# Linear attention and a mixture of experts on one core: unused keys left out, early chunks reordered, the expert choice and the small tiles' rows moved, last rows scaled by one engine

## The chip, the core and the metric

The kernel runs on one core of one Trainium2 chip. The time is device time in microseconds (us) from one launch; the median of several runs is compared. The engines of a core run their own queues of instructions in order: TensorE (PE; its weight loads are shown as PEld), VectorE (DVE), ScalarE (ACT), GpSimd (POOL) and SyncE (SP, which here issues nearly all transfers). An instruction that waits holds up everything behind it on its engine.

## The reference

Two stages, with the values of the first as the tokens of the second. First, causal linear attention with a decay per head (4 batches, 8 heads, 768 positions, 64 values a head):

```
for each block b of 64 positions:
    intra = ((qb @ kb.T) * Dmask) @ vb          # Dmask = lam ** (i - j), lower triangle
    inter = (qb * lam ** (pos + 1)) @ kv_state
    out[b] = intra + inter
    kv_state = lam ** 64 * kv_state + (kb * lam ** (63 - pos)).T @ vb
```

Then the 3072 tokens of 512 values go through 8 experts, each token through the one with the largest logit:

```
logits = x @ w_gate + modality_bias[modality_id]
e = argmax(logits);  gate = softmax(logits)[e]
out[token] = gate * (relu(x @ w1[e]) @ w2[e])    # w1: 512 x 1024, w2: 1024 x 512
```

## The kernel before

The attention works in chunks of 128 positions: 6 chunks a batch, 24 in all, taken in 12 pairs (pair m holds chunks 2m and 2m+1). `load(m)` brings the four inputs of a pair (keys turned, queries turned, values, keys in rows; 2 MB) into one of four buffers. For a chunk g, `scores` multiplies keys by queries for 8 heads, `mask` (L258, DVE, one instruction of 128x1024, tile `pt`) applies the decay, `query` (POOL) and `keys` (ACT, 8 small instructions, tile `kd`) scale queries and keys, `products` forms keys times values, `add` (DVE) rolls that into one of three states, `from_state` (L282) multiplies the scaled queries by the state, `values` (L293) the masked scores by the values, and ACT copies the result to `xt`. The last chunk of a batch (g % 6 == 5) has no `keys`, `products` and `add`, since no later chunk needs its state. `from_state` takes a list of chunks and steps through the head pairs p; for each p it does each chunk in turn, and `place` gives even and odd chunks opposite halves of the output's partitions, so that two chunks' four matmuls of 64x64 (one for each half of the heads) stand in four different quarters of the array:

```
        for p in range(NP):
            for g in both:
                if g % NC > 0:
                    for hl, r in enumerate(halves2):
                        nc.tensor.matmul(ops[g][place(g, hl), p, :], state[g % NC % 3][r, p, :], qds[g][r, p, :], ...
```

The results of `from_state` and of `turn` (L314, which transposes four chunks' `xt` into token rows, `grp`) share two PSUM buffers named `o`: a buffer is written again only when DVE (L321) and ACT (L323, two copies) have emptied it.

After pairs 3, 7 and 11 the routing of 8 chunks is made: `gates` (PE) gives logits, `gate_rows` (L358, DVE) transposes them, `choose` (L363) puts eight small instructions in a list `todo` (add the bias, maximum, two comparisons `eq`, `m8`, the one-hot `oh`, a subtraction, an exponential on ACT), and `do(n)` issues the next n of that list at fixed places. `ranks` (L381, PE) multiplies the one-hot by a triangle; its results give each token its slot, and POOL scatters the token rows to their experts' stretches of an array `placed`.

The second stage takes tiles of 256 tokens of one expert. `fetch_x`, `fetch_w1`, `fetch_w2` issue the transfers; `turn_rows` and `split_rows` (DVE, ACT) transpose a tile's rows (`xt`) and split them into a high and a low part; `split_w1` splits the first weights (`w1h` on ACT, `w1l` on DVE); `first_layer` multiplies on PE and splits the second weights meanwhile; `second(n, t)` does the second layer for half a tile, scales by the gate and scatters to the output. Tiles 0 to 3 come from early lists, tiles 6 to 13 are the fixed ones of the last list. Two small tiles (4 with up to 64 tokens, 5 with up to 32) are fitted in between: their rows are fetched (`xq`), turned by `thin_rows` (L630, DVE, tile `xf`, then one instruction for addresses, `to`), multiplied by `thin_first` (L727, PE, L737) between `second(n, 0)` and `second(n, 1)` of tiles 7 and 9, turned by `thin_turn` and finished by `thin_second` (PE, L764) inside the next tile's `first_layer`. PE, DVE, ACT and SP run in the order in which the code calls; POOL's order is tied by hand as well.

Of the kernel before, what the change touches and what calls it, by code (L numbers as in the profile page):

```python
# [18 lines left out]
NC = S // P  # L19
# [24 lines left out]
def linear_attention_moe(tc, qkv, lam, modality, wg, mbias, w1, w2, out):  # L44
    nc = tc.nc
    with ExitStack() as ctx:
# [38 lines left out]

        def load(m):
            halves[m] = slot([P, 4, HB, H * D], F32, "load")
            if m > 2:
                nc.sync.dma_start(out=halves[m], in_=source(m))
                return  # L90
            for c in range(HB):
                for part in ((slice(0, 2), slice(2, 4)) if m < 2 else (slice(0, 4),)):
                    nc.sync.dma_start(out=halves[m][:, part, c], in_=source(m)[:, part, c])

        for m in range(3):
# [121 lines left out]
        def query(g):  # L217

            if g % NC > 0:
                qds[g] = work.tile([P, NP, P], F32, name="qd", bufs=4)  # L220
                op = pool(nc.gpsimd.tensor_tensor(out=qds[g], in0=loaded(g)[1], in1=pq, op=ALU.mult))
                if g in begun:
                    after(op, begun.pop(g))
# [129 lines left out]
        def do(n=None):  # L353
            for what, args, kw in todo[:n]:
                what(*args, **kw)
            del todo[:n]
# [345 lines left out]
                                               op0=ALU.max, op1=ALU.subtract)  # L702
                between(i)

        def second(n, t, ticks=(1, 3, 5, 7), halved=False):
            idx = idxs[n]
            ts = slice(t * P, (t + 1) * P)
            yp = ps.tile([P, DM], F32, name="o", bufs=2)
            for f in range(FC):
                a, b = divmod(f, 2)  # L710
                mm = three(yp, hh[a // 2][:, a % 2, b, ts], hl[a // 2][:, a % 2, b, ts], w2h[a][:, b, :], w2l[a][:, b, :],
                           f == 0, f == FC - 1)
                if f in ticks:
                    tick(mm)
            y = work.tile([P, DM], F32, name="y", tag="qd", bufs=4)
            share = idx[:, t, 1:2].bitcast(F32)
            w = DM // 2 if halved else DM
            nc.scalar.activation(out=y[:, :w], in_=yp[:, :w], func=AF.Copy, scale=share)  # L718
            if halved:
                nc.vector.tensor_scalar(out=y[:, w:], in0=yp[:, w:], scalar1=share, scalar2=None, op0=ALU.mult)  # L720
            sc = nc.gpsimd.indirect_dma_start(  # L721
                out=out, out_offset=bass.IndirectOffsetOnAxis(ap=idx[:, t, 0:1], axis=0),
                in_=y, in_offset=None, bounds_check=N - 1, oob_is_err=False)
            apart("tokens", sc)
            pool(sc, free=True)
# [109 lines left out]
        scores(3)  # L835
        mask(3)
        query(3)
        gpsimd_constants()
        load(SLOTS)
        products(2)  # L840
        products(3)
        add(2)
        add(3)
        from_state((2, 3))
        values(2)
        values(3)
        block(4)
        turn(0, 0)
        turn(0, 1)
# [3 lines left out]
        turn(0, 3)  # L853
        load(1 + SLOTS)
        products(4)
        products(5)
        add(4)
        for m in range(2, pairs):
            a, b = HB * m, HB * m + 1
            ahead = m + 1 < pairs  # L860
            add(b)
            if ahead:
                block(a + 2)
                mm = block(b + 2)
                if m > 4:
                    tick(mm)
            if m == 2:
                routing_constants()
            elif m == 3:
                clear(slice(E * CAP, E * CAP + TT), TT)  # L870
            do(7)
            from_state((a, b))
            values(a)
            mm = values(b)
            if m == 5 or m == 9:
                jobs += [("slots", one_slot)] * RC
# [19 lines left out]
            if m % 2 and ahead:  # L896
                mm = turns(m // 2)
                if m > 4:
                    tick(mm)
            if m == 3 or m == 7:  # L900
                routed = m // 4, *choose(m // 4, gate_rows())
            do(3 + m % 2)
            if m == 8:
                need("slots")
                raw1 = w1_part("raw1", F32)
# [103 lines left out]
        for n in [3] + list(range(wides, fixed_ones)):  # L1009
            first_layer(between)  # L1010
            between = lambda i: None
            m = n + 1 if n > 3 else wides
            if m < fixed_ones:
                fetch_w2(*fetch_regs(m, m == wides))
                turn_rows(m)
                split_rows()
                if m + 1 < fixed_ones:
                    fetch_x(m + 1)
                split_w1()
                if m + 1 < fixed_ones:  # L1020
                    fetch_w1(*fetch_regs(m + 1))
            thin = {wides + 1: thins, wides + 3: thins + 1}.get(n)
            if thin:
                thin_rows(thin)
            second(n, 0)
            if thin:
                hn = thin_first(xf[thin], homes[thin][0])
            second(n, 1, halved=n + 1 == fixed_ones)
            if thin:
                hnt[thin] = thin_turn(hn)  # L1030
                between = finish(thin, 0)
            thin = {wides: thins, wides + 2: thins + 1}.get(n)
            if thin:
                fetch_x(thin)
                fetch_w1(*fetch_regs(thin, True), to=homes[thin][0])
                fetch_w2(*fetch_regs(thin, True), to=homes[thin][1])
# [68 lines left out]
```

## Time and profile before

| what | value |
|---|---|
| median of 3 runs | 407.89 us (405.15 to 409.21) |
| profiled execution, its own time | 407.92 us |
| its span (first to last instruction) | 406.2 us |
| PE busy | 385.9 us (95%) |
| DVE / ACT / POOL busy | 258.5 (64%) / 210.8 (52%) / 97.9 us (24%) |
| mean granted TensorE clock | 0.978 of full speed |
| moved by DMA | 83.77 MB, mean 206 GB/s |

The span is cut into stages with different limits, so the shares of busy time are averages. PE counts as busy while a matmul runs at whatever clock the throttle grants; a stretch at half clock is therefore not seen as idle. The view of waits tells for whom an engine sat idle; the timeline gives instructions in order of time with the idle time just before them and what ended it; the chain of waits follows the work back from the last instruction. In all of them an fp32 matmul leaves two records, so 8 instructions show as x16.

### The profile page before, as it was taken

The numbers are of one execution on the slowest core, as the hardware profiler recorded it, in microseconds if no ns is written. First come the engines' busy times: TensorE is split into PE (matmuls) and PEld (weight loads), VectorE is DVE, ScalarE is ACT, GpSimd is POOL, SyncE is SP. The second block draws the span as 40 slices with busy tenths as digits, with TensorE's granted clock in tenths as the row PEclk, the third lists the DMA queues.
The fourth block names the chain that finished last, engine by engine and source line by source line (L and its number), as shares of the span: only waits on it lengthen the run. The fifth ranks groups of instructions, "written<-read, shape, count | busy, mean of one in ns | idle before, by whom it ended". The sixth has DMA issues, their size and how long they took to land.

```text
span 406.2 us, 9717 instructions
## 1 busy us (share of the span) xinstructions
PE 385.9 (95%) x3602; PEld 339.7 (84%) x3602; DVE 258.5 (64%) x462; ACT 210.8 (52%) x411; POOL 97.9 (24%) x128
## 2 busy tenths in 40 slices
PE   8999799999999999999999959999959999999993
PEld 4889689888888989898989937889839989898982
DVE  5676859778576788866776651475742666758520
ACT  2477468775356465654655442364533365556420
POOL 2653219645502274010202010002011020100201
PEclk9999989999999999999999979999989999999997
DMA  7999868999769973799328995452930120210101
GB/s 252 388 400 406 329 243 284 399 333 314 208 180 312 361 237 121 292 358 319 82 54 260 341 362 217 129 165 77 395 79 27 24 57 27 64 42 2 53 0 50
DMA packets 41384, 83.77 MB, mean 206 GB/s; under 512 B 7278, under 2 KB 20078, under 8 KB 41328
## 3 DMA queue, kind: packets, MB, share of 16 engines
q1 hardware_dynamic: 37408, 70.28, 51.8%
q0 software_dynamic: 3920, 12.78, 8.2%
q8 instruction: 30, 0.49, 0.5%
q14 instruction: 26, 0.21, 0.2%
HBM read 90.57 MB, written 17.84 MB: 267 GB/s over the span
## 4 chain that ended last, share of the span: by engine, by line
PE 43%; issue 33%; DMA 9%; POOL 4%; DVE 4%; ACT 3%; SPq 2%; POOLq 0%; ACTq 0%; DVEq 0%
DMA load<-in_qkv_dram 5%; PE s L254 4%; PE o L298 4%; PE o L673 4%; PE o L675 4%; PE o L674 4%; POOL out_dram L721 4%; PE o L290 2%; PE o L317 2%; PE s L675 2%; PE s L674 2%; PE s L673 2%; ACT w1h L581 2%; PE s L693 2%; PE kv L693 2%
## 5 line engine op out<-in xcount | busy, mean ns | idle before, releaser
L582 DVE TENSOR_TENSOR w2l<-raw,w2h 128x1024 fp32r<-128x1024 f32 x48 | 58.7, 1224 | 40.2 <-ACT w2h L581 40.2
L721 POOL DMA_INDIRECT out_dram<-y,idx x24 | 29.6, 1234 | 226.0 <-ACT y L718 207.4
L673 PE MATMUL o<-w2h,hh 128*128 128x512 f32 x192 | 75.6, 394 | 0.0
L674 PE MATMUL o<-w2l,hh 128*128 128x512 f32 x192 | 75.0, 390 | 0.0
L675 PE MATMUL o<-w2h,hl 128*128 128x512 f32 x192 | 74.8, 390 | 0.0
L582 DVE TENSOR_TENSOR w1l<-raw,w1h 128x1024 fp32r<-128x1024 f32 x44 | 51.5, 1220 | 2.0 <-ACT w1h L581 2.0
L581 ACT CAST w2h<-raw 128x1024 fp32r<-128x1024 f32 x48 | 49.9, 1040 | 0.0
L673 PE MATMUL kv<-xh,w1h 128*128 128x256 f32 x176 | 49.7, 283 | 0.0
L673 PE MATMUL s<-xh,w1h 128*128 128x256 f32 x176 | 49.6, 282 | 0.0
L674 PE MATMUL s<-xl,w1h 128*128 128x256 f32 x176 | 49.5, 281 | 0.0
L674 PE MATMUL kv<-xl,w1h 128*128 128x256 f32 x176 | 49.4, 281 | 0.0
L675 PE MATMUL s<-xh,w1l 128*128 128x256 f32 x176 | 49.4, 281 | 0.0
L675 PE MATMUL kv<-xh,w1l 128*128 128x256 f32 x176 | 49.4, 281 | 0.0
L673 PEld LDWEIGHTS o<-w2h,hh 128*128 128x128 f32 x192 | 36.2, 188 | 8.3 <-issue 1.2
L581 ACT CAST w1h<-raw 128x1024 fp32r<-128x1024 f32 x44 | 42.8, 1044 | 0.0
L675 PEld LDWEIGHTS o<-w2h,hl 128*128 128x128 f32 x192 | 36.2, 188 | 7.7
L674 PEld LDWEIGHTS o<-w2l,hh 128*128 128x128 f32 x192 | 36.2, 189 | 7.1
L718 ACT ACTIVATE y<-o,idx 128x512 f32<-128x512 f32 (+1 forms) x24 | 16.2, 675 | 42.3 <-PE o L675 36.8
L236 ACT ACTIVATE kd<-load,dk 128x64 f32<-128x64 f32 x144 | 35.7, 338 | 3.3 <-DMA load<-in_qkv_dram 3.2
L673 PEld LDWEIGHTS kv<-xh,w1h 128*128 128x128 f32 x176 | 33.3, 189 | 0.6 <-issue 0.6
L674 PEld LDWEIGHTS s<-xl,w1h 128*128 128x128 f32 x176 | 33.2, 189 | 0.4
L673 PEld LDWEIGHTS s<-xh,w1h 128*128 128x128 f32 x176 | 33.2, 189 | 0.3
(191 smaller groups left out, 645.1 us busy)
## 6 DMA issues: line engine op xcount, KB each, us to landing
raw<-in_w_dram SPq DMA_DIRECT2D x96, 512.0 KB
load<-in_qkv_dram SPq DMA_DIRECT2D x9, 2048.0 KB
both<-in_w_dram SPq DMA_DIRECT2D x16, 512.0 KB
xg<-placed SPq DMA_DIRECT2D x48, 128.0 KB
placed<-blank SPq DMA_DIRECT2D x9, 528.0 KB
load<-in_qkv_dram SPq DMA_DIRECT2D x8, 512.0 KB
load<-in_qkv_dram SPq DMA_DIRECT2D x2, 1024.0 KB
placed<-grp,sloti POOLq DMA_INDIRECT x24, 6.2
```

What stands on the lines that cost most here:

```text
L236: nc.scalar.activation(out=kds[g][:, p, hl, :], in_=kn[:, p, hl, :], func=AF.Copy, scale=dk[:, hl, p, P - 1 : P])
L254: mm = nc.tensor.matmul(scs[g][:, hl, p, :], kt[r, p, :], qt[r, p, :], start=True, stop=True)
L290: nc.tensor.matmul(ops[g][place(g, hl), p, :], state[g % NC % 3][r, p, :], qds[g][r, p, :], start=(p == 0), stop=False)
L298: mm = nc.tensor.matmul(op[place(g, hl), p, :], vt[:, (2 * p + hl) * D : (2 * p + hl + 1) * D], pt[:, hl, p, :], start=(c == 0 and p == 0) ...
L581: nc.scalar.copy(out=hi, in_=src)
L582: nc.vector.tensor_tensor(out=lo, in0=src, in1=hi.bitcast(F32), op=ALU.subtract)
L673: nc.tensor.matmul(out, ah, bh, start=first, stop=False)
L674: nc.tensor.matmul(out, ah, bl, start=False, stop=False)
L675: return nc.tensor.matmul(out, al, bh, start=False, stop=last)
L693: mm = nc.tensor.matmul(hp[:, j, :], raw1[i][:, kc, fs], xt2[:, kc, :], start=(kc == 0), stop=(kc == KC - 1))
L718: nc.scalar.activation(out=y[:, :w], in_=yp[:, :w], func=AF.Copy, scale=share)
L721: sc = nc.gpsimd.indirect_dma_start(out=out, out_offset=bass.IndirectOffsetOnAxis(ap=idx[:, t, 0:1], axis=0), in_=y, in_offset=None, bound ...
```

## The change

Five edits.

1. `load`: of a pair whose second chunk is the last of a batch (m = 2, 5, 8, 11) that chunk's keys in rows are left out (0.25 MB each); such a pair comes in two transfers, one a chunk, where pairs 5, 8 and 11 came in one.
2. Chunks 2 to 5: `from_state` and `values` of chunk 2 stand behind `products(2)`, those of chunk 3 behind `products(3)`, those of chunk 4 ahead of the scores of chunks 6 and 7, each chunk alone; chunk 5 follows these scores, alone too.
3. `gate_rows` and `choose` of the first two routings go from the end of pairs 3 and 7 to the head of pairs 4 and 8, and all of `choose` is issued behind the masks of the next two chunks; `do` counts change to fit.
4. `thin_rows` goes from behind the next tile's `turn_rows`, `split_rows` and `split_w1` to ahead of them.
5. The last half tile's scaling, which ACT and DVE shared by halves, is done whole by ACT.

```
 def load(m):
     halves[m] = slot([P, 4, HB, H * D], F32, "load")
-    if m > 2:
+    last = (HB * m + 1) % NC == NC - 1
+    if m > 2 and not last:
         nc.sync.dma_start(out=halves[m], in_=source(m))
         return
     for c in range(HB):
-        for part in ((slice(0, 2), slice(2, 4)) if m < 2 else (slice(0, 4),)):
+        for part in ((slice(0, 2), slice(2, 4)) if m < 2 else (slice(0, 4 - (last and c)),)):
...
-            share = idx[:, t, 1:2].bitcast(F32)
-            w = DM // 2 if halved else DM
-            nc.scalar.activation(out=y[:, :w], in_=yp[:, :w], func=AF.Copy, scale=share)
-            if halved:
-                nc.vector.tensor_scalar(out=y[:, w:], in0=yp[:, w:], scalar1=share, scalar2=None, op0=ALU.mult)
+            nc.scalar.activation(out=y, in_=yp, func=AF.Copy, scale=idx[:, t, 1:2].bitcast(F32))
...
+        products(2)
         gpsimd_constants()
         load(SLOTS)
-        products(2)
+        from_state((2,))
+        values(2)
+        add(2)
         products(3)
-        add(2)
+        from_state((3,))
+        values(3)
         add(3)
-        from_state((2, 3))
-        values(2)
-        values(3)
         block(4)
...
         products(4)
-        products(5)
         add(4)
+        from_state((4,))
+        values(4)
         for m in range(2, pairs):
             a, b = HB * m, HB * m + 1
             add(b)
+            if m == 4 or m == 8:
+                routed = m // 4 - 1, *choose(m // 4 - 1, gate_rows())
             if ahead:
                 block(a + 2)
                 mm = block(b + 2)
...
-            do(7)
-            from_state((a, b))
-            values(a)
+            do(9 if m % 4 == 0 else 8)
+            if m > 2:
+                from_state((a, b))
+                values(a)
+            else:
+                from_state((b,))
             mm = values(b)
...
-            if m == 3 or m == 7:
-                routed = m // 4, *choose(m // 4, gate_rows())
-            do(3 + m % 2)
+            else:
+                do(4)
...
         for n in [3] + list(range(wides, fixed_ones)):
             first_layer(between)
             between = lambda i: None
+            thin = {wides + 1: thins, wides + 3: thins + 1}.get(n)
+            if thin:
+                thin_rows(thin)
             m = n + 1 if n > 3 else wides
             if m < fixed_ones:
                 fetch_w2(*fetch_regs(m, m == wides))
                 turn_rows(m)
                 split_rows()
...
                 split_w1()
...
-            thin = {wides + 1: thins, wides + 3: thins + 1}.get(n)
-            if thin:
-                thin_rows(thin)
             second(n, 0)
```

What stands on the engines, in the order in which they run it. First VectorE around tile 7, before (`hl` is the low part of the hidden values, `xt`, `xl`, `w1l` belong to the next wide tile, `xf` and `to` to the small one):

```order
L701 SCALAR_TENSOR_TENSOR hl_1800<-kv,hh_1798 128x512
L661 STREAM_TRANSPOSE xt_128<-xg 128x4x4x32 x2
L582 TENSOR_TENSOR xl_131<-xt_128,xh_129 128x512
L582 TENSOR_TENSOR xl_132<-xt_128,xh_130 128x512
L582 TENSOR_TENSOR w1l<-raw_1412,w1h 128x1024 x4
L661 STREAM_TRANSPOSE xf_3492<-xq_3260 128x2x4x32
L638 TENSOR_SCALAR to_3494<-idx_3259,strip 128x1
```

and now:

```order
L702 SCALAR_TENSOR_TENSOR hl_1802<-kv,hh_1800 128x512
L662 STREAM_TRANSPOSE xf_3421<-xq_3263 128x2x4x32
L639 TENSOR_SCALAR to_3423<-idx_3262,strip 128x1
L662 STREAM_TRANSPOSE xt_128<-xg 128x4x4x32 x2
L583 TENSOR_TENSOR xl_131<-xt_128,xh_129 128x512
L583 TENSOR_TENSOR xl_132<-xt_128,xh_130 128x512
L583 TENSOR_TENSOR w1l<-raw_1416,w1h 128x1024 x4
```

The two instructions of the small tile moved ahead of the eight of the next wide tile. The same move stands at tile 9.

Second, VectorE at the head of pair 4, before (`lgt` are the transposed logits, `state` the additions of `add(9)`, `pt` the masks of chunks 10 and 11, `m` and `oh` the end of the choice):

```order
L360 STREAM_TRANSPOSE lgt<-x 128x256
L355 TENSOR_TENSOR l<-lgt,bias 128x64
L355 TENSOR_REDUCE mx<-l 128x8
L355 TENSOR_TENSOR eq<-l,mx 128x64
L355 TENSOR_TENSOR eq<-eq,desc 128x64
L278 SCALAR_TENSOR_TENSOR state_122<-state_121,pq,kv 128x64 x4
L260 TENSOR_TENSOR pt<-s,dk 128x1024 x2
L355 TENSOR_REDUCE m_734<-eq 128x8
L355 TENSOR_TENSOR oh<-eq,m_734 128x64
```

and now:

```order
L279 SCALAR_TENSOR_TENSOR state_122<-state_121,pq,kv 128x64 x4
L361 STREAM_TRANSPOSE lgt<-x 128x256
L261 TENSOR_TENSOR pt<-s,dk 128x1024 x2
L356 TENSOR_TENSOR l<-lgt,bias 128x64
L356 TENSOR_REDUCE mx<-l 128x8
L356 TENSOR_TENSOR eq<-l,mx 128x64
L356 TENSOR_TENSOR eq<-eq,desc 128x64
L356 TENSOR_REDUCE m_739<-eq 128x8
L356 TENSOR_TENSOR oh<-eq,m_739 128x64
```

The state's additions moved ahead of the transposition, and the two masks ahead of the choice; nothing was added to or taken from the row that ends with `oh`.

Third, TensorE from the products of chunks 4 and 5 on, before (`kv` are products, `s` scores, `o` results with `qd,state` from the state and with `pt,load` from the values):

```order
L268 MATMUL kv<-load,kd 64x64 x8
L254 MATMUL s<-load 128x128 x16
L290 MATMUL o<-qd,state_122 64x128 x2
L290 MATMUL o<-qd,state_123 64x128 x2
...
L298 MATMUL o<-pt,load 64x128 x16
```

and now:

```order
L269 MATMUL kv<-load,kd 64x64 x8
L291 MATMUL o<-qd,state_122 64x128 x8
L299 MATMUL o<-pt,load 64x128 x8
L255 MATMUL s<-load 128x128 x16
L291 MATMUL o<-qd,state_123 64x128 x8
L299 MATMUL o<-pt,load 64x128 x8
```

Before, the two chunks' matmuls from the state alternated in pairs; now each chunk's eight stand together, and those of chunk 4 come ahead of the scores of chunks 6 and 7.

## Rows read from the trace of the kernel before

**Rows 1.** Waits of PE over the span: us in total, times, longest.

```profile
PE s L737 <- DVE xf L661: 8.7, 2, 4.4
PE x L382 <- DVE oh L355: 1.9, 1, 1.9
```

**Rows 2.** Windows: stretch, length, busy us (instructions) by engine, PEclk, DMA, GB/s.

```profile
50.55:53.96 3.41, 3.41 (x32) 3.34 (x32) 2.10 (x7) 3.41 (x13) 0.00 (x0) 0.50 1.02 416
239.38:245.11 5.73, 5.73 (x28) 3.26 (x30) 0.04 (x1) 0.00 (x0) 0.45 (x1) 0.50 1.11 301
299.72:303.13 3.41, 3.41 (x27) 1.75 (x20) 0.00 (x0) 0.38 (x1) 0.00 (x0) 0.50 0.21 77
```

**Rows 3.** Timeline, PE, small tiles: start, us, instruction, idle before and its releaser.

```profile
239.38 6.48 PE L737 MATMUL s<-both,xf 128*64 128x256 f32 x32 [4.42 <-DVE xf L661]
...
251.37 0.60 PE L748 MATMUL x<-ident,hn 128*128 128x128 f32 x4
...
254.71 3.67 PE L764 MATMUL o<-both,hnt 128*64 128x256 f32 x32
...
299.06 3.06 PE L737 MATMUL s<-both,xf 128*32 128x256 f32 x32 [4.28 <-DVE xf L661]
```

**Rows 4.** Timeline, DVE, around tile 7's end.

```profile
230.22 0.69 DVE L701 SCALAR_TENSOR_TENSOR hl<-kv,hh 128x512 fp32r<-128x512 f32 x1 [0.68 <-ACT hh L700]
...
238.89 0.44 DVE L661 STREAM_TRANSPOSE xf<-xq 128x256 f32<-128x256 f32 x1
```

**Rows 5.** Timeline, SP: issue of the small tile's rows.

```profile
217.87 2.54 SPq L600 DMA_DIRECT2D xq<-placed  x4
```

**Rows 6.** Chain of waits, 222 to 235: start, length, what (a transfer from issue).

```profile
224.60 6.22 DMA both<-in_w_dram
```

**Rows 7.** Timeline, DVE and POOL, the choice in pair 4.

```profile
44.09 2.51 POOL L221 TENSOR_TENSOR qd<-load,pq 128x512 f32<-128x512 f32 x2 [6.88 <-PE s L254]
...
44.48 0.97 DVE L355 TENSOR_TENSOR eq<-l,mx 128x64 f32<-128x64 f32 x1
...
45.55 1.13 DVE L355 TENSOR_TENSOR eq<-eq,desc 128x64 f32<-128x64 f32 x1
...
49.87 0.22 DVE L355 TENSOR_TENSOR oh<-eq,m 128x64 bf16<-128x64 f32 x1
```

**Rows 8.** Timeline, DVE, the same comparison in pair 8.

```profile
77.73 0.23 DVE L355 TENSOR_TENSOR eq<-l,mx 128x64 f32<-128x64 f32 x1
```

**Rows 9.** Timeline, POOL and DVE, masks of chunks 8 and 9.

```profile
34.70 2.51 POOL L221 TENSOR_TENSOR qd<-load,pq 128x512 f32<-128x512 f32 x2 [3.68 <-PE s L254]
34.82 2.35 DVE L260 TENSOR_TENSOR pt<-s,dk 128x1024 f32<-128x1024 f32 x2
```

**Rows 10.** Timeline, PE, DVE and ACT, chunks 2 to 7.

```profile
15.98 1.74 PE L268 MATMUL kv<-load,kd 128*64 128x64 f32 x32
...
17.65 1.62 PE L290 MATMUL o<-qd,state 64*64 64x128 f32 x32
...
26.58 1.27 DVE L321 COPY grp<-o 64x512 f32<-64x512 f32 x2
...
27.28 1.24 ACT L323 COPY grp<-o 64x256 f32<-64x256 f32 x4 [1.89 <-DVE grp L321]
...
27.60 2.06 PE L254 MATMUL s<-load 64*128 64x128 f32 x32 [0.57 <-DMA load<-in_qkv_dram]
```

**Rows 11.** Chain of waits, pairs 2 and 3.

```profile
29.65 1.03 PE o L290 x32
30.68 1.90 PE o L298 x32
...
35.50 1.02 PE o L290 x16
```

**Rows 12.** Page, costliest groups: busy us, mean ns | idle before, releaser.

```profile
L718 ACT ACTIVATE y<-o,idx 128x512 f32<-128x512 f32 (+1 forms) x24 | 16.2, 675 | 42.3 <-PE o L675 36.8
```

**Rows 13.** Timeline, DVE, the last half tile.

```profile
400.33 0.48 DVE L720 TENSOR_SCALAR y<-o,idx 128x256 f32<-128x256 f32 x1 [10.04 <-ACT y L718]
```

More of the change, by code (lines that the diff above doesn't have):

```diff
@@ L703, in first_layer, with second @@
                 between(i)
-        def second(n, t, ticks=(1, 3, 5, 7), halved=False):
+        def second(n, t, ticks=(1, 3, 5, 7)):
             idx = idxs[n]
@@ L1027, in linear_attention_moe @@
                 hn = thin_first(xf[thin], homes[thin][0])
-            second(n, 1, halved=n + 1 == fixed_ones)
+            second(n, 1)
             if thin:
```

## The prediction

> **What bounds the kernel now.** PE is busy for 95% of the span, so I read first for whom it waits, then the granted clock, since a PE at half clock also counts as busy. The waits of PE over the whole span have two entries of weight: 8.7 us in two pieces for `xf`, the small tiles' turned rows, and 1.9 us in one piece for `oh`, the one-hot of the choice [rows 1]. Other work of PE follows without a gap worth naming, so PE's queue sets the end and what it no longer waits for leaves the span, unless something else is late in its place. Then the windows: granted clock 0.50, which is the 1.2 GHz level, stands in three stretches inside the kernel, each right behind one of these waits: 50.55 to 53.96, 239.38 to 245.11 and 299.72 to 303.13 [rows 2]. PE was busy through all three. At the 2.4 GHz level the same matmuls take half, so these stretches hold 1.7, 2.9 and 1.7 us beyond the waits. The pool from which the change can draw is thus 8.7 + 1.9 + 6.3 = 16.9 us. Where DMA limits anything is one place, 0.57 us ahead of the scores of chunks 6 and 7 [rows 10].
>
> **The small tiles' rows.** DVE is done with tile 7's last `hl` at 230.9 and turns `xf` at 238.89 only, behind the next tile's transposition, splitting and four weight splits [rows 4]. PE had come to the small tile's matmuls 4.42 us before 239.38, the second time 4.28 us before 299.06 [rows 3]. With `xf` (0.44 us) and its address instruction (an estimate of 0.2, by the 0.23 of a small DVE instruction [rows 8]) at the head, `xf` is there at about 231.4 and PE comes to it at 234.96. Both waits go. Is the clock given back? The first small tile's 32 matmuls took 6.48 us, 32 of the same shape in `thin_second` at the upper level 3.67 [rows 3]; with no wait ahead I take the clock as kept: -2.9 for the stretch at 239 and -1.7 for that at 299, half of their busy time [rows 2]. Together -(4.42 + 4.28 + 2.9 + 1.7) = -13.3. What could take the wait's place is the small tile's weights: the last of four pieces of `both` is the chain's transfer, issued at 224.60 and landed 6.22 later, at 230.8 [rows 6], 4 us before PE comes. The rows `xq` were issued earlier on the same queue, 217.87 [rows 5]. What is delayed is the next wide tile's splitting, by 0.6, from 238.9 [rows 4] to 239.5. PE needs it for that tile's first layer, which began behind the transposition at 251.37 [rows 3] and now begins some 7.3 earlier, at 244.4: cover of 4.9 us, so nothing. If that cover were gone it would cost 0.6 each. Bounds: -8.7, if the clock drops all the same, to -13.4.
>
> **The choice.** The order of DVE's work changes, its sum ahead of `oh` does not. What changes is what runs beside it. The two comparisons took 0.97 and 1.13 us while POOL scaled queries from 44.09 to 46.60 [rows 7]; in pair 8, with POOL idle, the same comparison took 0.23 [rows 8]. Now the masks stand there. Two masks took 2.35 us with such a POOL stretch beside their whole length [rows 9], so I count them as 2.35 in either place. The comparisons then run after 46.6, beside nothing. So `oh`, done at 50.09 [rows 7], comes 0.97 + 1.13 - 0.46 = 1.64 earlier, and PE's 1.9 shrinks to about 0.3. I take -1.6, and the half clock behind it goes too: -1.7. Behind the wait of 0.57 two chunks' scores took 2.06 [rows 10], too short for half clock; behind the 1.9 the two chunks' scores lie in a stretch at 0.50 [rows 2]. Sum -3.3. Bounds: 0, if the comparisons stay as long behind the masks, to -3.6. Pair 8 had no wait for `oh` [rows 1]; its masks still go first, and its six small instructions of about 0.25 end close to where they did, so 0.
>
> The Trainium skill ("SBUF — State Buffer", section "SBUF: two separate sides") says that a VectorE instruction with two SBUF inputs and a GpSimd instruction that reads SBUF exclude each other for the whole instruction, and does not list one with an input from PSUM, as the masks have. The rows agree: 0.23 becomes 0.97 and 1.13, and the masks beside POOL stay at 1.17 each. By a plain sum of instructions, without such an exclusion, `oh` would come when it came before and this edit would bring 0.
>
> **Chunks 2 to 5.** This edit pays on one side and gains on the other. Eight matmuls from the state of one chunk alone hold PE for 1.02 us, the sixteen of two alternating chunks for 1.03 [rows 11]. So each pair that is taken apart costs 1.0 us more of PE.
> For chunks 2 and 3 this lies in idle time: their products took 1.74 and their state matmuls 1.62 [rows 10], where 1.03 is the unhindered time of the latter [rows 11] and, as an estimate by these rows, some 1.0 that of the former; 1.3 us were waits for `kd` of chunk 3, for the second state and for an `o` buffer. In the new order chunk 2's results fill them. About -0.15 net.
> For chunks 4 and 5 it does not. Chunk 4's state matmuls now follow `products(4)` and need the `o` buffer of the third `turn`. That is emptied by the first half of DVE's copies from 26.58 and then by the first two of ACT's four from 27.28, thus at 27.28 + 0.62 = 27.9 [rows 10], now 27.75. PE, which was there at 27.03 (27.60 less 0.57), arrives near 26.9 and waits 0.85, where before it waited 0.57 for the load. From there: state 1.02, values 0.95, scores of 6 and 7 2.06, state 1.02, values 0.95, end at 33.75. Before: 30.68 + 1.90 = 32.58 [rows 11]. So +1.2. ACT adds a little: the copy of chunk 4's result now stands ahead of the 16 scalings of keys 6 and 7, which end up to 0.2 too late for `products(7)`. I take +1.3 for the whole edit. Bounds: -0.7 (single chunks cost half of a pair, and the load's wait goes) to +3 (both pairs pay in full, the wait for `o` and 0.5 for ACT on top).
>
> The Trainium skill ("TensorEngine Tiling (Array Packing)", section "Tiling Modes") says that tiles of 64x64 are four and work independently, in parallel. It speaks against this edit, which leaves two of the four unused; the 1.02 against 1.03 agrees. By a count of matmuls alone the edit would cost no PE time, and the sum would be about 1.3 lower.
>
> **The rest.** The last half tile: the DVE half of 0.48 began at 400.33 on ACT's half [rows 13], so the two stood one behind the other, about 0.96; whole on ACT it is 0.68 [rows 12]. -0.3; bounds 0 to -0.5. The keys left out: 1 MB of 84, of which 0.25 MB lies ahead of the load that PE waited for; that wait is already taken out above, and no later load is among PE's waits. The added transfers, one each for pairs 5, 8 and 11, stand on SP well ahead of need: 0.
>
> **Sum.** -13.3 - 3.3 + 1.3 - 0.3 = -15.6. The profiled execution took 407.92, practically the median of 407.89, so 392.3.
>
> **The rivals.**
> Small tiles still wait for something: one of the two stretches keeps its wait and half clock, because a transfer (weights, rows) is needed earlier than it lands. Against it: 4 us between the weights' landing and PE's coming [rows 3, 6]. Price 6 to 7.3 us: about 399.
> The choice gains nothing: something other than POOL stretched the comparisons, or a short wait still brings half clock. For it: only one pair shows the stretch. Time 392.3 + 3.3 = 395.6.
> The reorder costs nothing or gains: if ACT and the `o` buffers follow sooner than I worked out, 392.3 - 2.0 = 390.3. For it: the buffers' emptying hangs on DVE's second mask, which could move.
> Slower: `xf` now stands ahead of the next wide tile on an engine that runs in order, so if `xq` were not there at 230.9, DVE would stand still with 8 us of work for the next tile behind it. The cover of 4.9 us is used up when `xq` lands at 235.8; from there each us is a us, and 15.6 us later, past 251, the kernel is slower than before, for instance 410. Against it: `xq` is issued at 217.87, ahead of weights that land by 230.8 [rows 5, 6].
>
> **How the numbers follow.** All as summed, 0.70; one small tile still waits 0.08; the choice gains nothing 0.11; the reorder free 0.07; slower 0.04. The likeliest gives 392.3, by itself 390 to 395. Leaving out the first and the last rival (0.12) and the rim of the others, the range is 389.8 to 397.0. About 1% is what a measurement of this kernel tells from no change, 403.8 and 412.0. Faster by over 1% holds for all but the last rival (0.04, of which 0.01 ends within 1%) and a first one in which both small tiles wait (0.02, within 1%): 0.94; within 1% 0.03; slower 0.03.
>
> **What would show it.** In PE's waits of the changed kernel the entry for `xf` is gone and that for `oh` is under 0.6; no half clock between 10 us and the last matmul; the small tile's first layer takes about 3.6 and 1.8 us instead of 6.48 and 3.06; `eq` takes 0.23 in pair 4; the scores of chunks 8 and 9 begin near 34.8 instead of 33.5; the span is near 390.6. It is wrong if half clock stands somewhere new, if PE waits for `both` or if DVE waits for `xq`.

## The result, and the profile after

| | before | after |
|---|---|---|
| median | 407.31 us (405.15 to 409.21) | 393.12 us (393.02 to 395.74) |
| profiled execution, its own time | 407.92 us | 393.13 us |
| its span | 406.2 us | 391.4 us |
| PE busy | 385.9 us (95%) | 381.3 us (97%) |
| mean granted clock | 0.978 | 0.996 |

The ratio is 0.967, with a 95% interval of 0.961 to 0.973: 14.2 us faster, where 15.6 were predicted. Two later sets of runs gave 0.965 and 0.971 (below).

First PE's waits over the whole span (engine, line, tile, releaser: us in total, times, longest), the new one and the one that is left of those in the prediction:

```profile
PE o L291 <- ACT grp L324: 1.0, 1, 1.0
...
PE x L383 <- DVE oh L356: 0.2, 1, 0.2
```

The 8.7 us for `xf` of [rows 1] have gone altogether and the 1.9 for `oh` are 0.2. One wait of 1.0 is new: the `o` buffer ahead of chunk 4's state matmuls. Then the windows (columns as in [rows 2]):

```profile
10.00:50.00 40.00, 38.35 (x696) 33.93 (x693) 27.12 (x62) 24.45 (x87) 18.02 (x37) 1.00 0.98 364
50.00:100.00 50.00, 49.36 (x937) 44.02 (x937) 40.45 (x128) 36.44 (x123) 27.38 (x36) 1.00 0.94 324
100.00:230.00 130.00, 130.00 (x848) 118.05 (x847) 93.20 (x156) 70.39 (x97) 31.60 (x33) 1.00 0.73 236
230.00:300.00 70.00, 70.00 (x530) 59.82 (x529) 39.94 (x47) 35.06 (x47) 9.16 (x8) 1.00 0.67 220
300.00:385.10 85.10, 85.10 (x542) 77.23 (x541) 50.16 (x54) 41.39 (x54) 9.18 (x8) 1.00 0.12 36
388.28:391.40 3.12, 0.00 (x0) 0.00 (x0) 0.00 (x0) 0.00 (x0) 0.00 (x0) 0.50 0.05 17
```

The granted clock is at its upper level from 10 us to the last matmul; half clock stands only where PE has nothing left to do. From 100 us on PE is busy without a gap.

Where the time went, by stage. A stage begins with the first instruction named, in the timeline of each profiled execution; times in us:

| from, to | before | after | difference | predicted |
|---|---|---|---|---|
| scores of chunk 0, scores of chunk 8 | 27.83 | 29.59 | +1.8 | +1.3 (chunks 2 to 5) |
| scores of chunk 8, scores of chunk 14 | 27.80 | 24.61 | -3.2 | -3.3 (choice) |
| scores of chunk 14, first layer of tile 0 | 39.17 | 39.18 | 0.0 | 0 |
| first layer of tile 0, `hnt` of small tile 1 | 151.60 | 144.34 | -7.3 | -7.3 (4.42 + 2.9) |
| `hnt` of small tile 1, of small tile 2 | 56.52 | 50.71 | -5.8 | -6.0 (4.28 + 1.7) |
| `hnt` of small tile 2, end | 97.64 | 97.44 | -0.2 | -0.3 (last half tile) |

(`hnt` is DVE's copy of the small tile's turned hidden rows, behind its first layer.)

The small tiles in the timeline of after, DVE and PE (start, us, instruction, idle before):

```profile
229.30 0.43 DVE L662 STREAM_TRANSPOSE xf<-xq 128x256 f32<-128x256 f32 x1
...
233.36 3.67 PE L734 MATMUL s<-both,xf 128*64 128x256 f32 x32
...
286.03 1.93 PE L734 MATMUL s<-both,xf 128*32 128x256 f32 x32
```

None of them waits for anything. `xf` is done 3.6 us before PE wants it; the first layers take 3.67 and 1.93 us where [rows 3] has 6.48 and 3.06. The rows' transfer held up nobody.

The choice in pair 4, timeline of after, DVE, POOL and PE:

```profile
45.70 2.51 POOL L222 TENSOR_TENSOR qd<-load,pq 128x512 f32<-128x512 f32 x2 [6.87 <-PE s L255]
...
46.24 2.31 DVE L261 TENSOR_TENSOR pt<-s,dk 128x1024 f32<-128x1024 f32 x2
...
48.96 0.22 DVE L356 TENSOR_TENSOR eq<-l,mx 128x64 f32<-128x64 f32 x1
...
49.29 0.23 DVE L356 TENSOR_TENSOR eq<-eq,desc 128x64 f32<-128x64 f32 x1
...
50.08 0.19 PE L383 MATMUL x<-oh,lowb 128*128 128x64 bf16 x1 [0.24 <-DVE oh L356]
...
50.39 2.06 PE L255 MATMUL s<-load 64*128 64x128 f32 x32
```

The masks now stand beside POOL's queries (45.70 to 48.21) and take 2.31 us for two. POOL makes no difference to them: in before all 24 masks lie between 1.21 and 1.23 us each, whether POOL scaled queries beside them (34.82 [rows 9]) or not (47.37 to 49.71). Instructions by line, before (duration in ns: least, median, most):

```profile
L260 DVE TENSOR_TENSOR pt<-s,dk x24: 1206/1218/1225, 7.1 to 94.7; 128x1024 f32<-128x1024 f32 x24
```

The comparisons come behind the queries and take 0.22 and 0.23 against 0.97 and 1.13 [rows 7].

Chunks 4 to 7, timeline of after, PE:

```profile
28.05 1.09 PE L291 MATMUL o<-qd,state 64*64 64x128 f32 x16 [0.99 <-ACT grp L324]
29.07 1.09 PE L299 MATMUL o<-pt,load 128*64 128x128 f32 x16
30.09 2.06 PE L255 MATMUL s<-load 64*128 64x128 f32 x32
32.08 1.09 PE L291 MATMUL o<-qd,state 64*64 64x128 f32 x16
33.10 1.09 PE L299 MATMUL o<-pt,load 128*64 128x128 f32 x16
...
35.05 2.06 PE L255 MATMUL s<-load 64*128 64x128 f32 x32
```

Starts are what to read here: chunk 4's state matmuls hold PE for 1.02 us (28.05 to 29.07), chunk 5's for 1.02 again (32.08 to 33.10).

### The profile page after: what moved, and what is told of

Read it like the earlier page. It is cut to its first block, busy times and chain, and to the rows that moved or that the text cites. A ratio compares the mean times of both kernels' runs of the same rounds, so it can differ in the third digit from the quotient of the medians.

```text
span 391.4 us, 9713 instructions
## 1 busy us (share of the span) xinstructions
PE 381.3 (97%) x3602; PEld 337.5 (86%) x3602; DVE 256.8 (66%) x461; ACT 210.5 (54%) x411; POOL 98.3 (25%) x128
## 4 chain that ended last, share of the span: by engine, by line
PE 56%; issue 31%; POOL 4%; DMA 3%; DVE 3%; SPq 1%; ACT 1%; POOLq 0%; DVEq 0%
PE o L674 6%; PE o L676 6%; PE o L675 6%; PE s L255 5%; PE o L299 5%; POOL out_dram L718 4%; PE o L291 3%; PE kv L674 2%; PE s L676 2%; PE kv L675 2%; PE s L675 2%; PE s L674 2%; PE kv L676 2%; PE o L318 2%; DMA load<-in_qkv_dram 2%
## 5 line engine op out<-in xcount | busy, mean ns | idle before, releaser
L583 DVE TENSOR_TENSOR w2l<-raw,w2h 128x1024 fp32r<-128x1024 f32 x48 | 58.8, 1224 | 39.2 <-ACT w2h L582 38.1
L717 ACT ACTIVATE y<-o,idx 128x512 f32<-128x512 f32 x24 | 16.4, 684 | 40.4 <-PE o L676 34.6
```

Source lines behind the costliest of these rows:

```text
L583: nc.vector.tensor_tensor(out=lo, in0=src, in1=hi.bitcast(F32), op=ALU.subtract)
L717: nc.scalar.activation(out=y, in_=yp, func=AF.Copy, scale=idx[:, t, 1:2].bitcast(F32))
```

## Experiments

Theory: four causes that add up, each in its own stage: the late `xf` with half clock behind it; comparisons beside POOL's queries with half clock behind the wait for them; single chunks that use half of the array; the tail. Rivals are named with each run. A run is compared with the kernel before on the same chip.

**The small tiles: edit 4 undone in the changed kernel, and edit 4 alone.**

```
 # a_thin_back: the changed kernel, thin_rows behind split_w1 as before
 # b_thin_only: the kernel before with
             first_layer(between)
             between = lambda i: None
+            thin = {wides + 1: thins, wides + 3: thins + 1}.get(n)
+            if thin:
+                thin_rows(thin)
...
-            thin = {wides + 1: thins, wides + 3: thins + 1}.get(n)
-            if thin:
-                thin_rows(thin)
             second(n, 0)
```

> The changed kernel with thin_rows put back behind the next tile's splitting (edit 4 undone). My theory: PE waits 4.4 and 4.3 us for xf again and half clock stands behind both waits, so the time is 13.1 us longer than the changed kernel's, about 406.2, ratio to the kernel before 0.997. Rival (the waits return but the clock was lost for another reason and stays): 8.7 us longer, about 401.8. Rival (the gain came from elsewhere): about 393.

Measured: 407.81 us against 410.16, ratio 0.995 [0.993, 0.998]. Timeline, PE, and windows of this kernel:

```profile
239.95 5.36 PE L734 MATMUL s<-both,xf 128*64 128x256 f32 x32 [4.41 <-DVE xf L662]
...
298.68 3.58 PE L734 MATMUL s<-both,xf 128*32 128x256 f32 x32 [4.28 <-DVE xf L662]
```
```profile
240.62:244.04 3.42, 3.42 (x18) 1.95 (x16) 0.00 (x0) 0.00 (x0) 0.00 (x0) 0.50 1.15 278
298.65:302.06 3.41, 3.38 (x32) 1.38 (x32) 0.07 (x1) 0.00 (x0) 0.61 (x1) 0.50 0.40 116
```

Both waits are back, within 0.01 us, and half clock behind both. The first stretch of it is 3.4 us long here. In the profiled execution of before it is 6.8: the 5.73 of [rows 2] are the part in which PE was busy, and half clock had set in while PE still waited. A window of before:

```profile
238.50:239.38 0.88, 0.00 (x0) 0.00 (x0) 0.88 (x3) 0.00 (x0) 0.88 (x1) 0.50 1.01 400
```

> The kernel before with edit 4 alone: the small tiles' rows turned ahead of the wide tile's. Theory (the waits and both half-clock stretches behind them go, and nothing else depends on the other edits): 13.1 to 13.4 us less than before, a ratio of 0.967 to 0.968, no half clock between 230 and 310 us, the wait for xf gone. Rival (the small tiles only gain so much because the other edits bring them there at another time, or the clock falls again behind the 1.9 us wait of the choice and later): 8.7 us less, ratio 0.979, with half clock still behind the small tiles.

Measured: 396.08 us against 408.71, ratio 0.968 [0.963, 0.974], 12.6 us less. Timeline, PE:

```profile
235.42 3.67 PE L737 MATMUL s<-both,xf 128*64 128x256 f32 x32
```

The first small tile waits for nothing and runs at the upper level; no half clock stands between 230 and 310 us. By stages the two `hnt` come 7.26 and 5.82 us sooner than in the profiled execution of before, 13.1 in all, as in the changed kernel. Some 0.9 of these hang on that execution, with its long stretch of half clock: between the stages of a_thin_back, which has the short one, and those of the changed kernel it is 12.2. The rival (8.7 with half clock left) falls. This one move is worth nearly the whole change.

**Is half clock brought on by the wait?** The kernel before, with matmuls that nobody reads in place of PE's idle time:

```
+        def fill():
+            nothing = ps.tile([P, DM], F32, name="o", bufs=2)
+            for i in range(18):
+                nc.tensor.matmul(nothing, hh[0][:, 0, 0, :P], w2h[0][:, 0, :], start=(i == 0), stop=(i == 17))
...
             if thin:
+                fill()
                 hn = thin_first(xf[thin], homes[thin][0])
```

> The kernel before with 18 matmuls of 128x512 that nobody reads (0.226 us each, 4.1 us in all) put on TensorE between the second layer's first half and each small tile, where it waits for xf. The rows come no earlier, so the wait itself can't be won. Theory (half clock behind the wait is brought on by TensorE's idleness): idle time for xf falls from 4.4 and 4.3 to about 0.3 each, no half clock behind it, and the 2.9 and 1.7 us of it are won: 4.6 less than before, ratio 0.989. Rival (half clock has another cause, such as the load of the small tile's work or its shape): half clock stays at 239 and 299 us, ratio 1.0.

Measured: 405.56 us against 408.71, ratio 0.992 [0.990, 0.995]. Timeline, PE:

```profile
236.32 4.24 PE L1004 MATMUL o<-w2h,hh 128*128 128x512 f32 x18
240.89 3.67 PE L737 MATMUL s<-both,xf 128*64 128x256 f32 x32 [0.33 <-DVE xf L661]
...
297.91 1.93 PE L737 MATMUL s<-both,xf 128*32 128x256 f32 x32 [0.20 <-DVE xf L661]
```

The rows come no earlier, yet the small tiles' first layers take 3.67 and 1.93 us, as in the changed kernel, and their stages are 2.8 and 1.5 us shorter than in the profiled execution of before: 4.3 of the 4.6 expected. The median won 3.15, less. Two causes are likely and not shown for the executions that were only timed: some executions of before may lack the long stretch (a_thin_back shows one without), and the stage from chunk 14 to tile 0 takes 42.1 us in this profile, 39.2 in that of before (last section). The theory holds: PE's idleness brings half clock here, not the small tile's work.

**The choice: edit 3 undone, edit 3 alone, and its cause removed in another way.**

```
 # a_choice_back (changed kernel); b_choice_only is the reverse, in the kernel before
-            if m == 4 or m == 8:
-                routed = m // 4 - 1, *choose(m // 4 - 1, gate_rows())
...
-            do(9 if m % 4 == 0 else 8)
+            do(7)
...
-            else:
-                do(4)
+            if m == 3 or m == 7:
+                routed = m // 4, *choose(m // 4, gate_rows())
+            do(3 + m % 2)
```

> The changed kernel with the choice back at the end of pairs 3 and 7 and the old do counts (edit 3 undone). My theory: the two comparisons take 0.97 and 1.13 us beside POOL's queries, PE waits 1.9 us for oh, and the scores of chunks 12 and 13 run at half clock: 3.1 to 3.3 us longer than the changed kernel, about 396.3. Rival (the place of the choice does not matter; the shift by the reordered chunks took the wait away): 393.1.

Measured: 398.16 us against 410.16, ratio 0.973 [0.967, 0.978], where the changed kernel has 0.965 to 0.971: undoing the edit costs 0.7 to 3.3 us, and the trace has to say more. Timeline, DVE and PE, and a window:

```profile
46.27 0.96 DVE L356 TENSOR_TENSOR eq<-l,mx 128x64 f32<-128x64 f32 x1
...
47.34 1.13 DVE L356 TENSOR_TENSOR eq<-eq,desc 128x64 f32<-128x64 f32 x1
...
51.94 0.19 PE L383 MATMUL x<-oh,lowb 128*128 128x64 bf16 x1 [1.87 <-DVE oh L356]
```
```profile
52.24:55.70 3.46, 3.46 (x76) 3.17 (x74) 3.22 (x8) 3.44 (x14) 1.25 (x1) 1.00 1.05 405
```

The stretched comparisons and the wait are back, but not half clock: here PE runs at the upper level behind a wait of 1.87 us. b_thin_only and b_fill show the same wait, also without half clock. In all three the stage from chunk 8 to chunk 14 takes 26.3 us, against 27.80 in before and 24.61 in after. So 1.67 us of this edit are the wait, and 1.52 are half clock that only some executions have.

> The kernel before with edit 3 alone: the choice at the head of pairs 4 and 8, issued behind the masks. Theory (the comparisons no longer run beside GpSimd's queries, and nothing new does): the one-hot's wait is 0.2 to 0.3 instead of 1.9 and the stretch behind it is at full clock, so 1.6 to 3.3 us less than before, ratio 0.992 to 0.996, the lower end where an execution of before has half clock there at all; nothing of it is given back between 59 and 76 us. Rival (a gain there is given back as it was when GpSimd's queries were held back instead, 0.8 us in the median): ratio 0.998 and waits of TensorE for state at 66 to 70 us.

Measured: 405.32 us against 406.82, ratio 0.998 [0.993, 1.002], so not told from no change by itself. Its profile has the whole gain at its place: `oh` waited for 0.24, the stage at 24.61, the next one 39.17. But its ten executions lay in two groups, 403.7 to 406.1 and 408.4 to 410.3 us, so a second execution was profiled:

> The kernel before with edit 3 alone, a second execution of it. Of its ten timed executions six took 403.7 to 406.1 us at a mean granted clock of 0.986 to 0.989 and four 408.4 to 410.3 at 0.978. Theory (what differs is how long the clock is halved behind the same waits, and where): an execution near 408.5 has half clock in full behind both small tiles, or one stretch more in the attention, at the same instructions and waits as one near 404. Rival (a different wait, of its own): another entry among TensorE's waits, of 2 us or more. An execution near 404 again tells neither.

It took 406.86 us, between the groups. The stage from chunk 8 to 14 is as short as before (24.6), but the next is 2.3 us longer, with two new waits, 0.55 for the state at 69.57 and 1.86 for `grp` at 74.14; waits of PE, and the timeline of DVE and POOL:

```profile
PE o L317 <- ACT grp L323: 2.1, 2, 1.9
```
```profile
65.43 3.24 DVE L355 TENSOR_SCALAR listA<-atA 128x2 int32<-128x2 f32 x1
...
66.12 2.50 POOL L221 TENSOR_TENSOR qd<-load,pq 128x512 f32<-128x512 f32 x2
```

An instruction of two values a partition (0.16 us in the first execution) ends at 68.67, just behind POOL's two query instructions (68.62). It began 0.7 us ahead of them, so the collision alone doesn't say why it hadn't ended by then. Half clock differs too: at the first small tile it is 6.8 us long here, in part while PE was idle, and 3.4 in the first execution, and the stage up to that tile's `hnt` takes 151.26 for 150.50; at the second tile both have 3.4. So both the rival's wait and the theory's longer half clock are there.

```
 # b_hold: the kernel before, POOL's queries of chunks 10 and 11 wait for the second comparison
+                if g == 10 or g == 11:
+                    after(op, done[3])
```

(`done` holds what `do` has issued of the choice; its fourth entry is the second comparison.)

> The kernel before with nothing moved, but POOL's queries of chunks 10 and 11 wait for the second comparison, so that they no longer run beside the two comparisons. My theory (POOL's instruction holds up the comparisons): both take 0.23 us, oh comes 1.6 us earlier, PE's wait for it falls from 1.9 to about 0.3 us, no half clock at 50 us, and the time is 3.2 us shorter than the kernel before, ratio 0.992. Rival (the comparisons are long for another reason, such as the transposed input): they stay at 0.97 and 1.13 and the time is that of the kernel before, ratio 1.000.

Measured: 408.72 us against 410.16, ratio 0.998 [0.995, 1.001]. Timeline, DVE, POOL and PE, and a window:

```profile
44.55 0.22 DVE L357 TENSOR_TENSOR eq<-l,mx 128x64 f32<-128x64 f32 x1
...
45.34 2.52 POOL L221 TENSOR_TENSOR qd<-load,pq 128x512 f32<-128x512 f32 x2 [8.05 <-DVE eq L357]
...
59.51 2.51 POOL L221 TENSOR_TENSOR qd<-load,pq 128x512 f32<-128x512 f32 x2
...
59.93 2.16 DVE L357 TENSOR_SCALAR deltaA<-ntA 128x8 f32<-128x8 f32 x1
...
65.92 2.49 POOL L221 TENSOR_TENSOR qd<-load,pq 128x512 f32<-128x512 f32 x2 [0.38 <-PE s L256]
...
67.32 1.11 DVE L357 CAST listA<-firstA 128x2 int32<-128x2 f32 x1
...
68.76 1.65 PE L292 MATMUL o<-qd,state 64*64 64x128 f32 x28 [1.97 <-DVE state L280]
```
```profile
69.14:72.56 3.42, 3.42 (x46) 3.09 (x39) 3.42 (x11) 0.20 (x1) 0.93 (x2) 0.50 0.99 394
```

With POOL held back the comparisons take 0.22: it was POOL that stretched them. And the gain is lost 15 us later: now the two small instructions at 59.9 and 67.3 meet POOL's next queries (2.16 and 1.11 us; 0.17 and 0.34 in before), PE waits 1.97 for the state, and half clock stands behind that. The stage from chunk 8 to 14 is as short as in the changed kernel (24.64), the next takes 44.1 us where before has 39.2. Of the expected 3.2 the medians show 1.4, which the interval doesn't tell from nothing.

**Chunks 2 to 5 as pairs again.**

```
 # a_pair45: chunks 4 and 5; a_order_back: also 2 and 3
         products(4)
+        products(5)
         add(4)
-        from_state((4,))
-        values(4)
...
-            if m > 2:
-                from_state((a, b))
-                values(a)
-            else:
-                from_state((b,))
+            from_state((a, b))
+            values(a)
```

> The changed kernel with chunks 4 and 5 back as a pair (from_state((4, 5)) behind the scores of chunks 6 and 7), chunks 2 and 3 left as changed. My theory: two chunks' matmuls from the state take 1.03 us again instead of 2 x 1.02 and the wait of 0.99 for the o buffer goes, so the scores of chunks 8 and 9 begin at 33.5 instead of 35.05 and the time is 1.6 us shorter, about 391.5. Rival (the reorder helps, because the load of pair 3 is waited for in the old place): same or up to 0.6 longer than 393.1. Rival (the loss at 35 us is taken up later by a wait that is there anyway): same as the changed kernel, 393.1.

Measured: 392.74 us against 410.16, ratio 0.961 [0.954, 0.968]. The scores of chunk 8 begin at 32.86, where 33.5 was expected and the changed kernel has 35.05. The changed kernel was not timed on that chip; with the fuller version it was:

> The changed kernel with all of edit 2 undone: chunks 2 and 3, and 4 and 5, again as pairs. Theory (single chunks cost TensorE 1.0 us more for each pair; for 4 and 5 it stands on the path, for 2 and 3 it is filled by idle time): 1.6 less than the changed kernel beside it, the same as where only 4 and 5 were put back, or up to 0.15 more; scores of chunks 8 and 9 begin near 32.9 instead of 35.05. Rival (the earlier gain there is given back in the pairs up to the placing of the first list, 59 to 76 us, where VectorE and GpSimd meet anew): 0.4 less or nothing, though the scores of chunks 8 and 9 are early.

> The changed kernel itself, unchanged, on the chip of the runs beside it, so that the others have a level to be held against. No theory disputes it: a ratio of about 0.967 to the kernel before, whatever the chip's own level (394 us where the kernel before takes 408, 396.5 where it takes 410). If the ratio is lower here, near 0.96, chips differ in what the change is worth and not only in their level.

Measured on one chip, before at 408.71: all pairs back 393.52 us (392.57 to 393.88), ratio 0.961 [0.955, 0.967]; the changed kernel 394.93 us (394.75 to 395.04), ratio 0.965 [0.959, 0.970]. 1.4 us, and the two groups of four don't overlap: **undoing edit 2 wins about what the edit was predicted to cost, and the change without it beats both kernels.** Both profiles have the longer form of the stage from chunk 14 to tile 0 (41.07 and 40.98), so that doesn't make the difference. Timeline, PE, of a_order_back:

```profile
29.59 1.10 PE L291 MATMUL o<-qd,state 64*64 64x128 f32 x32
30.62 1.97 PE L299 MATMUL o<-pt,load 128*64 128x128 f32 x32
...
33.45 2.06 PE L255 MATMUL s<-load 64*128 64x128 f32 x32
```

Both chunks' state matmuls take 1.03 us together (29.59 to 30.62). From the scores of chunk 0 to those of chunk 8 it is 27.0 us, against 29.5 in the changed kernel and 27.8 in before. Why 2.5 in the profile and 1.4 in the median: this execution's first scores began 0.8 us later than the other's. Most of the 0.8 by which it beats before at this place is the load's wait of 0.57 [rows 10], which is gone: the scores of chunks 6 and 7 begin at 27.01 in a_pair45, at 27.60 in before, and at 27.66 and 27.70 in b_choice_only and b_thin_only, which load all keys. So edit 1 seems to bring some 0.6 where chunks 4 and 5 stay a pair (not tried by itself); in the changed kernel PE stands at the `o` buffer at that time.

**Edits 1 and 5 undone, beside the changed kernel once more.**

```
-            last = (HB * m + 1) % NC == NC - 1
-            if m > 2 and not last:
+            if m > 2:
...
-                for part in ((slice(0, 2), slice(2, 4)) if m < 2 else (slice(0, 4 - (last and c)),)):
+                for part in ((slice(0, 2), slice(2, 4)) if m < 2 else (slice(0, 4),)):
...
-            second(n, 1)
+            second(n, 1, halved=n + 1 == fixed_ones)
```

> The changed kernel with edits 1 and 5 undone: the unused keys are loaded again and the last half tile is scaled by ACT and VectorE by halves. Theory: the two halves again stand one behind the other, 0.2 to 0.3 more at the end; the keys are worth nothing, since no later load is among TensorE's waits: 0.2 to 0.4 us more than the changed kernel beside it. Rival (the 0.25 MB that no longer lies ahead of the load of chunks 6 and 7 is worth part of TensorE's 0.57 us wait for it): 0.5 to 0.9 more, and a wait for the load at 27 to 30 us that the changed kernel has not.

> The changed kernel once more, as the level beside which the two other runs of this chip are held. About 0.966 of the kernel before. The profile also shows whether the 1.3 us by which the stretch between the scores of chunks 16 and 17 and those of 18 and 19 differed (8.97 us in the first profile of the changed kernel, 10.23 in the second) comes and goes with the chip: no theory of the change says that it should.

Measured: 394.11 us (393.48 to 398.0) against 394.19 (393.07 to 397.19): no difference that this can tell. DVE's half again stands behind ACT's:

```profile
385.78 0.47 ACT L718 ACTIVATE y<-o,idx 128x256 f32<-128x256 f32 x1 [4.75 <-PE o L675]
386.29 0.48 DVE L720 TENSOR_SCALAR y<-o,idx 128x256 f32<-128x256 f32 x1 [10.04 <-ACT y L718]
```

that is 0.99 us in a row, where the changed kernel has one ACT instruction of 0.69: 0.3, as worked out, and no more than the spread. The rival's wait for the load doesn't appear; in this kernel PE stands at the `o` buffer for 0.99 at that place, which would cover it.

## Why the prediction was right, step by step

**Small tiles: -13.3 predicted, -13.1 measured.** Both waits and all half clock behind them went; the wide tile's splitting, 0.6 later, delayed nobody. b_thin_only gives this part by itself (12.6 in the median), and b_fill shows that the half-clock share is a consequence of the wait. The rival of a transfer that is late and the one of a DVE that stands still did not occur: nothing stands in front of `xf` at 229.30.

**Choice: -3.3 predicted, -3.2 in the profile.** Masks ahead of comparisons cost the masks nothing, and the comparisons are short again. Right in place and, for this pair of traces, in size; but half of it, the half clock, rests on one execution. Three other executions with the same wait ran at the upper level, so the sure part is 1.7. The prediction took one profile's clock as the kernel's. In medians the edit alone was not told from no change (b_choice_only). The Trainium skill ("SBUF — State Buffer", section "SBUF: two separate sides") has the port pair that VectorE and GpSimd share as an exclusive lock, held for the whole instruction by whichever starts first, and names as takers VectorE instructions in a mode that uses two ports or with two SBUF inputs. In b_hold two with one input are held too: `deltaA` ends at 62.09 and POOL's queries at 62.02, the cast at 68.43 and the queries at 68.41; which mode they ran in no row shows.

**Chunks 2 to 5: +1.3 predicted, +1.6 to +1.8 measured.** The scores of chunk 8 began at 35.05 where 34.8 was predicted. Single chunks cost 1.02 for 1.03, as argued. Off were small terms that mostly cancel: PE waited 0.99 for the buffer (0.85 predicted) and started at 28.05 (27.75); chunks 2 and 3 gave nothing (-0.15 predicted: scores of chunk 4 at 21.13, before 21.10); ACT's 0.2 did not occur (products of 6 and 7 follow the values at once). The rival that the reorder is free falls. The Trainium skill ("TensorEngine Tiling (Array Packing)", section "Tiling Modes"), by which four tiles of 64x64 can work at once, agrees with 1.02 for one chunk and 1.03 for two.

**Tail: -0.3 predicted, -0.2 measured; rest 0.** As worked out.

**Total.** In the profiles -14.8 against -15.6: 0.5 less from chunks 2 to 5, 0.2 from the small tiles, 0.1 each from choice and tail; the first scores began 0.15 sooner. In the median the gain is 13.8 (after_again) and 12.6 us (after_third), also because executions differ: before's in half clock, which the prediction counted in full, and those of both kernels in the stage from chunk 14 to tile 0 (last section; 1.8 us more in the profile of after_again). Of its markers all appeared: no `xf` among the waits, `oh` at 0.2, full clock throughout, 3.67 and 1.93 us, `eq` 0.22; the span is 391.4 for 390.6.

## What to carry to other kernels

When an engine waits for a small result, look at what the producing engine does just before it: the rows were there, their 0.4 us instruction stood behind 8 us of work for a later consumer. Where half clock stands behind a wait, count it with the wait, but as a part that only some executions have, and look at more than one profile before putting it in full. A small instruction that takes several times its usual duration is a sign of a second engine beside it: move the pair apart, but check where the other engine's next long instruction will land.

## What was not expected of the hardware

**GpSimd's long instructions hold up more than comparisons.** Beside its scaling of queries a VectorE instruction on eight values a partition, with one input, took 2.16 us instead of 0.17 and a cast of two values 1.11 instead of 0.34 (b_hold). The stage from chunk 14 to tile 0 takes 39.2 us in some executions and 41 in others, with the change or without (after 39.18, after_third 39.17, before 39.17; after_again 40.98, b_thin_only 41.07), and in after_again such a meeting is part of it. Timeline, POOL and DVE, first of after, then of after_again, with PE's wait behind it:

```profile
62.11 2.52 POOL L222 TENSOR_TENSOR qd<-load,pq 128x512 f32<-128x512 f32 x2
...
63.98 0.68 DVE L356 TENSOR_SCALAR deltaA<-ntA 128x8 f32<-128x8 f32 x1
```
```profile
62.64 2.53 POOL L222 TENSOR_TENSOR qd<-load,pq 128x512 f32<-128x512 f32 x2
...
64.07 1.14 DVE L356 TENSOR_SCALAR deltaA<-ntA 128x8 f32<-128x8 f32 x1
...
72.40 0.86 DVE L279 SCALAR_TENSOR_TENSOR state<-state,pq,kv 128x64 f32<-128x64 f32 x4 [1.46 <-PE o L318]
...
74.57 1.25 PE L318 MATMUL o<-ident,xt 128*128 128x128 f32 x8 [0.74 <-ACT grp L324]
```

POOL starts its queries 0.5 us later, `deltaA` ends with them (65.2) and not at 64.7, and all behind it slides by 0.5. That is not what makes the difference in general: `deltaA` took 0.17 in b_thin_only (41.07) and 1.33 in a_loads_tail_back (39.18). What the six executions at 41 us (after_again, b_thin_only, a_thin_back, a_choice_back, a_order_back, a_pair45) share, and the five at 39.2 (before, after, after_third, b_choice_only, a_loads_tail_back) lack, is two waits of PE: 0.7 to 0.9 for `grp` ahead of the scores of chunk 18, and 0.6 to 0.8 for the state shortly before tile 0 (0.65 at 97.77 in after_again). Ahead of the first the state addition starts late: at 72.40 here, 0.9 us after the products that it needs, where in after it follows by 0.1. The row names PE's transposition L318 as what it waited for, whose result the addition doesn't read, so the cause stays open.

**Half clock is not a fixed consequence of a short wait.** Behind 4.4 and 4.3 us of idleness at the small tiles it came in all five profiled executions that had them (before, a_thin_back, b_hold, both of b_choice_only), for 3.4 us or about twice that; behind the choice's 1.9 us in one of four (before; not in a_choice_back, b_thin_only, b_fill). Behind 1.97 for the state in b_hold it came, behind 1.86 for `grp` in b_choice_again it did not. What decides at about 1.9 us no run here shows.
